# Whole first key transfer, modulation in rows, two-step picks and an early deal in a decode-attention kernel

## The chip, the cores and the metric

The kernel runs on one core of one Trainium2 chip. The time is the device time of one execution in microseconds; the median over the runs shown counts. Three runs of the kernel before gave 663.67 to 663.97, median 663.8.

## The reference

One decoding step of a transformer block with adaptive layer norm, for 4 sequences (B) and one new token each. D is 512, there are 32 heads (H) of 128 (Dh), and the caches hold 4096 keys and values for each sequence and head. All tensors are bf16.

```python
mod = (silu(c) @ w_mod).reshape(4, 6, 1, 512)          # sa, ca, ga, sb, cb, gb
h = layernorm(x) * (1 + ca) + sa
q = (h @ wq).reshape(B, 1, H, Dh).transpose(0, 2, 1, 3)
p = softmax(einsum('bhqd,bhkd->bhqk', q, k_cache) * Dh ** -0.5)
o = einsum('bhqk,bhkd->bhqd', p, v_cache)
x = x + ga * (o.reshape(B, 1, H * Dh) @ wo)
h = layernorm(x) * (1 + cb) + sb
z = gelu(h @ w_in);  z1, z2 = z[..., :896], layernorm(z[..., 896:])
x = x + gb * ((z1 * (w_sp * z2 + b_sp)) @ w_out)       # w_sp and b_sp are one number each
```

Keys and values are 134 MB each; with the weights the core reads 282.73 MB.

## The kernel before

**Stages.** The prologue loads wq and five of the six sections of w_mod, works out the modulation, the first layer norm and all queries, and spreads these so that each partition holds the query of its own head. The loop then runs over 32 sets, i = 0 to 31 (NT; L is the last, N0 = 30). Sets 0 to 29 are pairs: two sets share 8 heads of one sequence ; K and V of such a pair are 8.39 MB each, an even set and the odd one after it being the two halves of the keys. The last two sets hold four heads each of the last sequence. An epilogue projects with wo, does the second norm and the gated MLP, and writes 4 KB.

**A set.** A set has 128 keys per partition. `mult(i, 0)` and `mult(i, 1)` multiply a half of the key tile by the query in place on VectorE (L387). `reduce_d` sums over Dh with 16 matmuls against an identity on TensorE (L395), or with 4 for a part of the second half, and `sum8` finishes the sum on VectorE (L418); `sum_rest` does the remaining 48 keys on VectorE alone (L407). `scores` finds the maximum and calls `exps`, eight exponentials on ScalarE (L461) that write the weights `pbd`. `pv` multiplies them with V (64 matmuls, L516) into PSUM tile `ops`, where each partition holds results for G = 4 key groups side by side, of which a mask `sel` picks the right one: `o_pick` does this with one multiply and three multiply-adds (L525, L529). `o_cols` turns the result, `o_scale` divides by the sum of the weights and writes `oTp`.

**Buffers and the queue.** K tiles alternate between SBUF buffers A and B, V always goes into C. At the start C holds wq, w_mod and the small tiles of the prologue; so the first V load waits until the prologue has read all of them, the last being the two scalars `sp_t` (w_sp and b_sp, loaded by ScalarE's queue at L338 and L339 behind the last query copy, and read by the matmul at L362 in `late_mod_b`). SP issues all other loads, in the order of the code: wq, w_mod, K0 (two halves), K2, then V1, K4, V3, K6 and so on; a transfer named K4 holds sets 4 and 5, and V3 goes with sets 2 and 3. A V load waits for the `pv` before it, a K load for the last `sum_rest` in its buffer. At the end come wo, V30, the last V in four pieces (TAIL = 64, 32, 16, 16 keys), the last section of wo (`wol`, two halves), w_in, w_out and the last section of w_mod (`KG`, three pieces). Loads share eight semaphores, so a load also waits for the one eight places before it.

**Order.** The order of instructions on each engine is that of the code (a manual schedule). `late_mod_b` stands after the first `reduce_d` and before `mult(0, 1)`:

```python
        reduce_d(i, 0)
        ...
        if i == 0:
            late_mod_b()
        ...
        mult(i, 1)
```

`mod_cols` makes the modulation of the first two sections in columns: for each of 8 blocks, four matmuls with a strided block of w_mod as the weights. `late_mod_a` makes three more in rows (cT as the weights, 512 columns, one section on each group of 32 rows), copied to `mrows`; `late_mod_b` turns them.

**The end.** `deal(k)` spreads the `oTp` of a group of 8 heads over the partitions with eight matmuls, `dealt(k)` masks and sums on VectorE; `project` multiplies the first three groups by wo, `turn` turns the result, and `project_last` does the last group once set L is done. `o_last` runs the last V piece by piece: part 0 through `ops`, the others straight into the columns that `o_first` adds the picked part to. The epilogue's last step multiplies the MLP result `tt` by gb, whose matmuls (L872) need the last piece of w_mod.

Of the kernel before, what the change touches and what calls it, by code (L numbers as in the profile page):

```python
# [8 lines left out]
BF16 = mybir.dt.bfloat16  # L9
F32 = mybir.dt.float32  # L10
AF = mybir.ActivationFunctionType
ALU = mybir.AluOpType
AX = mybir.AxisListType
# [3 lines left out]
HP = 8  # L17
KC = 64
RD = 8
TAIL = (64, 32, 16, 16)  # L20
KIN = (slice(0, 2), slice(2, 4))
KG = (slice(0, 2), slice(2, 3), slice(3, 4))
JW = (slice(0, 4), slice(4, 7))
RW = (slice(0, 4), slice(4, 8))

# [26 lines left out]
def kernel(  # L52
# [16 lines left out]
    nc = tc.nc  # L69
    P = 128  # L70
    B, _, D = A_x.shape
# [3 lines left out]
    DJ = D // P  # L75
# [33 lines left out]
    def ps_sm(shape, dtype=F32):  # L109
        return psum.tile(shape, dtype, name="sm", bufs=3)  # L110

    def ps_q():
        return psum.tile([P, 512], F32, name="qps", bufs=1)
# [13 lines left out]
    def kv_view(cache, i):  # L127
        if i < N0:
            g, b = divmod(i // 2, B)
            v = cache[b, g * HP:(g + 1) * HP]  # L130
        else:
            h0 = GP * HP + (i - N0) * HQ
            v = cache[BL, h0:h0 + HQ]
        v = v.rearrange("h s d -> (h s) d")
        return v.rearrange("(p n) d -> p n d", p=P)
# [4 lines left out]
    def load(dst, src, cuts):  # L140
        n0 = 0
        for n in cuts:
            nc.sync.dma_start(out=dst[:, n0:n0 + n, :], in_=src[:, n0:n0 + n, :])
            n0 += n

    def load_k(i):
        if i < N0:
            load(bufs[i // 2 % 2], kv_view(A_k_cache, i), (NJ, NJ) if i == 0 else (NP,))
        else:
            load(kts[i], kv_view(A_k_cache, i), (KC, NJ - KC) if i == L else (NJ,))  # L150

    def load_v(i):
        if i < N0:
# [55 lines left out]
    def bc(ap, n):  # L209
        return ap[:, None, :].to_broadcast([P, n, ap.shape[-1]])  # L210
# [52 lines left out]
    nc.vector.reciprocal(out=sg, in_=sg)  # L263
    nc.vector.tensor_tensor(out=cT, in0=cx, in1=sg, op=ALU.mult)

    def mod_cols(s0, n, dst):

        for m in range(n):
            s, j = divmod(m, DJ)
            c0 = (s0 + s) * D + j  # L270
            for k in range(DJ):
                nc.tensor.matmul(  # L272
                    dst[:, m, :], lhsT=wm_sb[:, k, c0:c0 + (P - 1) * DJ + 1:DJ], rhs=cT[:, k, :],
                    start=(k == 0), stop=(k == DJ - 1),
                )

    xps = rows_to_cols(x_sb)
    xT = consts.tile([P, DJ, B], F32, name="xT")
# [1 line left out]
    xc1, rs1 = normed(pre, xT, "ln1")  # L280
    xn = pre.tile([P, DJ, B], F32, name="xn")
    nc.vector.tensor_tensor(out=xn, in0=xc1, in1=bc(rs1, DJ), op=ALU.mult)
    modA = ps_sm([P, 2 * DJ, B])
    mod_cols(0, 2 * DJ, modA)
    hs = pre.tile([P, DJ, B], F32, name="hs")
    nc.vector.scalar_tensor_tensor(  # L286
        out=hs, in0=modA[:, DJ:2 * DJ, :], scalar=1.0, in1=xn, op0=ALU.add, op1=ALU.mult
    )
    hT = pre.tile([P, DJ, R], BF16, name="hT")
    nc.gpsimd.memset(hT, 0.0)  # L290
    nc.vector.tensor_tensor(out=hT[:, :, 0:B], in0=hs, in1=modA[:, 0:DJ, :], op=ALU.add)

    GQ = 4
    ib = ident_bf.rearrange("p (q r) -> p r q", r=R)[:, 0:B, :, None]
# [42 lines left out]
    sp_t = pre.tile([1, 2], BF16, name="sp_t")  # L337
    nc.scalar.dma_start(out=sp_t[:, 0:1], in_=B_w_sp[0:1, 0:1])  # L338
    nc.scalar.dma_start(out=sp_t[:, 1:2], in_=B_b_sp.rearrange("(a b) -> a b", b=1))  # L339
    mrows = pre.tile([P, D], F32, name="mrows")  # L340
    nc.gpsimd.memset(mrows, 0.0)
    modT = consts.tile([P, 3 * DJ, B], F32, name="modT")
    g8 = consts.tile([P, 2, B], F32, name="g8")
    spf = consts.tile([P, 2], F32, name="spf")

    def late_mod_a():
        mp = ps_sm([P, D])
        for k in range(DJ):
            for s in range(3):
                nc.tensor.matmul(  # L350
                    mp[R * s:R * s + B], lhsT=cT[:, k, :], rhs=wm_sb[:, k, (2 + s) * D:(3 + s) * D],
                    start=(k == 0), stop=(k == DJ - 1), tile_position=(0, R * s),
                )
        for s in range(3):
            nc.scalar.copy(out=mrows[R * s:R * s + B], in_=mp[R * s:R * s + B])

    def late_mod_b():
        mps = ps_sm([P, DJ, 3 * R])
        for j in range(DJ):
            nc.tensor.transpose(mps[:, j, :], mrows[0:3 * R, j:D:DJ], ident_f[0:3 * R, 0:3 * R])  # L360
        sps = ps_sm([P, 2])
        nc.tensor.matmul(sps, lhsT=ones_b, rhs=sp_t, start=True, stop=True)  # L362
        nc.vector.tensor_copy(  # L363
            out=modT.rearrange("p (s j) b -> p s j b", s=3),
            in_=mps.rearrange("p j (s r) -> p s j r", s=3)[:, :, :, 0:B],
        )
        nc.vector.tensor_copy(out=spf, in_=sps)
        nc.gpsimd.tensor_copy(out=g8[:, 1, :], in_=spf[:, 0:1].to_broadcast([P, B]))
        cbT = modT[:, 2 * DJ:3 * DJ, :]
        nc.gpsimd.tensor_scalar_add(out=cbT, in0=cbT, scalar1=1.0)  # L370

    cbT = modT[:, 2 * DJ:3 * DJ, :]
    late_mod_a()

    st = {}
    oTp = consts.tile([P, NT // 2, HP], BF16, name="oTp")
# [120 lines left out]
    def norm_b(i):  # L497
        if (i, "z") in st:
            z = st.pop((i, "z"))
            rz = wk.tile(list(z.shape), F32, name=f"rz{z.shape[1]}", bufs=2 if pair(i) else 4)  # L500
            nc.vector.reciprocal(out=rz, in_=z)
            st[i, "rz"] = rz
# [8 lines left out]
    def pv_some(i, m0, m1, end):  # L511
        pb, vt, rows = (pbd8, bufC, G * HP) if pair(i) else (pbds[:, i % 4], vts[i], G * HQ)
        for m in range(m0, m1):
            n = slice(m * G, (m + 1) * G)
            g = R * (m % 4)
            nc.tensor.matmul(  # L516
                ops_of(i)[g:g + rows], lhsT=pb[:, n, :], rhs=vt[:, n, :],
                start=(m < 4), stop=(m >= end - 4), tile_position=(0, g),
            )

    def o_pick(i):
        ops = ops_of(i)
        sel = sels[HP if pair(i) else HQ]
        osb = wk.tile([P, DH], F32, name="osb", bufs=2)
        nc.vector.tensor_scalar(  # L525
            out=osb, in0=ops[:, 0, :], scalar1=sel[:, 0:1], scalar2=None, op0=ALU.mult
        )
        for g in range(1, G):
            nc.vector.scalar_tensor_tensor(  # L529
                out=osb, in0=ops[:, g, :], scalar=sel[:, g:g + 1], in1=osb,  # L530
                op0=ALU.mult, op1=ALU.add,
            )
        st[i, "osb"] = osb

    def o_cols(i):
# [7 lines left out]

    def o_last(i, part):
        n0, n1 = sum(TAIL[:part]), sum(TAIL[:part + 1])
        if part == 0:
            pv_some(i, 0, n1 // G, n1 // G)
            return
        if part == 1:
            st[i, "op"] = psum.tile([P, HQ], F32, name="qps", bufs=1)  # L550
        for k in range(n0, n1):
            nc.tensor.matmul(
                st[i, "op"], lhsT=vts[i][:, k, :], rhs=pbds[:, i % 4, k, :],
                start=(part == 1 and k == n0), stop=(k == NJ - 1),
            )

    def o_first(i):
# [30 lines left out]
    NL = GP * HP * DH  # L588

    def load_wo():  # L590
        nc.sync.dma_start(
            out=wo_sb.rearrange("p (k r) n -> p k r n", r=HP),
            in_=A_wo[0:NL].rearrange("(k p r) n -> p k r n", k=GP, p=P),
        )

    def load_end():
        wol = A_wo[NL:H * DH].rearrange("(p r) n -> p r n", p=P)
# [22 lines left out]
            in_=ident_bf.rearrange("p (u r) -> p r u", r=HP)[:, :, None, :].to_broadcast([P, HP, HP, P // HP]),  # L620
        )

    def deal(k):
        pp = ps_sm([P, HP, B, HP])
        for r in range(HP):
            nc.tensor.matmul(
                pp[:, r], lhsT=spot[:, r, :], rhs=oTp[:, k * B:(k + 1) * B, :], start=True, stop=True,
            )
        st["pp", k] = pp

    own = late.tile([P, HP * B, HP], F32, name="own")

    def dealt(k):
        pp = st.pop(("pp", k))
        nc.vector.tensor_tensor(
            out=own, in0=pp.rearrange("p r b h -> p (r b) h"), in1=bc(mask8, HP * B), op=ALU.mult,
        )
        od = late.tile([P, HP, B], BF16, name=f"od{k}")
        with nc.allow_low_precision("all but one term of each sum are zero"):
            nc.vector.tensor_reduce(  # L640
                out=od.rearrange("p r b -> p (r b)"), in_=own, axis=AX.X, op=ALU.add
            )
        st["od", k] = od

    accR = qbp[0:B].rearrange("b g n d -> b (g n d)")[:, 0:2 * D].bitcast(F32)

# [14 lines left out]
    def turn():  # L661
        wp = ps_sm([P, DJ, B])
        for j in range(DJ):
            nc.tensor.matmul(
                wp[:, j, :], lhsT=accR[:, j:D:DJ], rhs=ident_f[0:B, 0:B], start=True, stop=True,
            )
        return wp
# [95 lines left out]
    )  # L763
    for i in (N0, L):
        norm_b(i)
    wp = turn()
    nc.vector.tensor_tensor(out=acc, in0=wp, in1=gaT, op=ALU.mult)
    x1 = x1w[:, :, 0:B]
# [1 line left out]
    nv = NJ // G  # L770
    pv_some(N0, 0, nv // 4, nv)
    xc = centred(tl, x1, "ln2", lambda: pv_some(N0, nv // 4, nv, nv))
    o_last(L, 0)
    o_pick(N0)
    o_cols(N0)
# [4 lines left out]
    o_first(L)  # L780
    o_last(L, 3)
    o_scale(L)
    deal(GP)
    dealt(GP)
    wp = project_last()
    last = tl.tile([P, DJ, B], F32, name="last")
    nc.vector.tensor_tensor(out=last, in0=wp, in1=gaT, op=ALU.mult)
# [82 lines left out]
    for k in range(DJ):  # L870
# [23 lines left out]
    )  # L894
    tt = tl.tile([P, B, DJ], F32, name="tt")
    nc.vector.tensor_tensor(out=tt, in0=t3[:, 0], in1=t3[:, 1], op=ALU.add)
    nc.vector.tensor_scalar(
        out=t3[:, 2], in0=yb[:, 0], scalar1=spf[:, 1:2], scalar2=None, op0=ALU.mult
    )
    nc.vector.tensor_tensor(  # L900
        out=tt, in0=tt, in1=rs3[:, :, None].to_broadcast([P, B, DJ]), op=ALU.mult
    )
# [37 lines left out]
```

## Time and profile before

| | |
|---|---|
| runs, median | 663.67 to 663.97, 663.8 us |
| profiled execution | 663.61 us, span 661.8 us |
| granted TensorE clock, mean | 0.745 |
| VectorE busy | 570.6 us, 86% |
| TensorE matmul busy | 313.0 us, 47% |
| ScalarE busy | 170.9 us, 26% |
| DMA | 283.07 MB in 8188 packets, mean 428 GB/s |
| chain that ended last | DMA 62%, VectorE 21%, TensorE 11%, ScalarE 4% |
| VectorE waiting for K at L387 | 25.0 us (buffer A) and 13.6 us (buffer B) |

The span is the time from the first to the last instruction of the profiled execution; the time of the run is 1.8 us more. The chain is followed back from the last instruction to what released each step, so its shares tell where waiting was, not where an engine was busy. A row of the timeline gives start, duration, engine, line, operation, tiles and shapes, the number of instructions, and in brackets the idle time before and what ended it. A load's wait counts from its issue to its landing, so it has the time in line behind other loads in it.

### The profile page before, as it was taken

How to read it: one execution, taken by the hardware profiler on the slowest of the kernel's cores; microseconds unless marked ns; L12 is line 12 of the kernel's file. 1: busy time of each engine (PE TensorE's matmuls, PEld its weight loads, DVE VectorE, ACT ScalarE, POOL GpSimd, SP SyncE). 2: the span in 40 equal slices, each digit the busy share in tenths (PEclk: the TensorE clock that was granted, in tenths of full speed). 3: DMA queues.
4: the chain of work that ended last, by engine and by line, in shares of the span. 5: the costliest groups of instructions: out<-in, count | busy, mean ns of one | idle time of the engine just before them, and what ended most of it. 6: DMA issues, size and time to landing. Idle time of an engine off the chain costs nothing.

```text
span 661.8 us, 5160 instructions
## 1 busy us (share of the span) xinstructions
PE 313.0 (47%) x2100; PEld 134.7 (20%) x2100; DVE 570.6 (86%) x400; ACT 170.9 (26%) x282; POOL 23.9 (4%) x56
## 2 busy tenths in 40 slices
PE   1554454536153453625346361543635154363896
PEld 0221121212021121202112120111212021121345
DVE  3249999999898998989899897989989898999934
ACT  1210605032060603206060320605023060503222
POOL 3020000000000000000000000000000000030100
PEclk9988786866678786667877666787757678776876
DMA  8999999999999999999999999999999999999996
GB/s 364 449 425 444 440 441 440 441 401 440 445 428 440 437 436 416 445 436 428 437 440 433 428 440 429 424 444 440 429 432 437 424 440 445 416 415 454 412 421 280
DMA packets 8188, 283.07 MB, mean 428 GB/s; under 512 B 860, under 2 KB 1380, under 8 KB 2916
## 3 DMA queue, kind: packets, MB, share of 16 engines
q1 hardware_dynamic: 8144, 282.73, 99.0%
q8 instruction: 16, 0.26, 0.1%
q14 instruction: 8, 0.07, 0.0%
q10 hardware_dynamic: 20, 0.01, 0.0%
HBM read 282.73 MB, written 0.00 MB: 427 GB/s over the span
## 4 chain that ended last, share of the span: by engine, by line
DMA 62%; DVE 21%; PE 11%; ACT 4%; issue 1%; POOL 0%; SPq 0%; ACTq 0%; DVEq 0%
DMA bC<-in_A_v_cache_dram 34%; DMA bA<-in_A_k_cache_dram 19%; DVE bA L387 9%; DVE S L407 7%; PE ops L516 7%; DMA bC<-in_w_mod_dram 4%; DMA bC<-in_A_wo_dram 4%; ACT pbd L461 3%; PE red L395 2%; DVE S L418 2%; DMA bC<-in_B_b_sp_dram 1%; DVE bB L387 1%; PE qps L322 1%; PE sm L314 1%; DVE osb L529 0%
## 5 line engine op out<-in xcount | busy, mean ns | idle before, releaser
L461 ACT ACTIVATE pbd<-S,nb 32x256 bf16<-32x256 f32 x120 | 154.3, 1520 | 425.5 <-DVE nb L448 424.3
L387 DVE TENSOR_TENSOR bA<-bA,qbp 128x8192 bf16<-128x8192 bf16 x32 | 142.7, 4459 | 25.0 <-DMA bA<-in_A_k_cache_dram 25.0
L395 PE MATMUL red<-bB,ident_bf 128*128 128x512 bf16 x344 | 95.3, 435 | 117.5 <-DVE bB L387 117.5
L395 PE MATMUL red<-bA,ident_bf 128*128 128x512 bf16 x332 | 93.9, 442 | 116.8 <-DVE bA L387 116.8
L395 PEld LDWEIGHTS <-ident_bf 128*128 128x128 bf16 x676 | 72.5, 109 | 347.5 <-issue 183.4
L387 DVE TENSOR_TENSOR bB<-bB,qbp 128x8192 bf16<-128x8192 bf16 x28 | 123.7, 4417 | 13.6 <-DMA bB<-in_A_k_cache_dram 13.6
L516 PE MATMUL ops<-bC,pbd 128*32 128x512 bf16 x960 | 82.5, 519 | 68.8 <-DMA bC<-in_A_v_cache_dram 63.7
L407 DVE TENSOR_REDUCE S<-bA 128x48 f32<-128x6144 bf16 x15 | 98.1, 6542 | 0.0
L407 DVE TENSOR_REDUCE S<-bB 128x48 f32<-128x6144 bf16 x14 | 91.6, 6541 | 0.0
L516 PEld LDWEIGHTS <-pbd 128*32 128x32 bf16 (+1 forms) x1008 | 36.9, 125 | 116.5 <-issue 60.6
L461 ACT ACTIVATION_READ_ACCUMULATOR pbd<-S,nb 32x1 f32 x120 | 58.7, 489 | 0.0
L418 DVE TENSOR_REDUCE S<-red 128x64 f32<-128x512 f32 x64 | 43.7, 683 | 4.0 <-PE red L395 3.8
L475 POOL TENSOR_TENSOR rsb<-maskd,rs 128x8 f32<-128x8 f32 x15 | 3.9, 260 | 557.6 <-ACT pbd L461 557.6
L387 DVE TENSOR_TENSOR bB<-bB,qbo 128x8192 bf16<-128x8192 bf16 x4 | 17.6, 4410 | 0.0
L529 DVE SCALAR_TENSOR_TENSOR osb<-ops,m,osb 128x128 f32<-128x128 f32 x45 | 15.8, 351 | 1.6
L494 PE MATMUL sm<-rsb,inv_d 128*128 128x32 f32 (+2 forms) x12 | 3.1, 358 | 14.4 <-POOL rsb L475 14.4
L461 ACT ACTIVATE pbd<-S,nM 32x128 bf16<-32x128 f32 x8 | 4.6, 577 | 13.7 <-POOL pbd L707 12.5
L286 DVE SCALAR_TENSOR_TENSOR bC<-sm,bC 128x16 f32<-128x16 f32 x1 | 0.2, 175 | 8.6 <-PE sm L272 8.6
L431 DVE TENSOR_REDUCE mrow<-S 128x1 f32<-128x256 f32 (+1 forms) x17 | 6.9, 404 | 0.6
L363 DVE COPY modT<-sm 128x48 f32<-128x48 f32 x1 | 0.2, 207 | 7.3 <-PE sm L360 7.3
L322 PE MATMUL qps<-bC 128*128 128x256 bf16 (+1 forms) x16 | 4.5, 383 | 4.1 <-ACT qbp L332 2.8
L618 POOL COPY bA<-ident_bf 128x1024 bf16<-128x1024 bf16 x1 | 6.2, 6211 | 0.0
(160 smaller groups left out, 140.0 us busy)
## 6 DMA issues: line engine op xcount, KB each, us to landing
bA<-in_A_k_cache_dram SPq DMA_DIRECT2D x2, 4096.0 KB, 32.0
bC<-in_A_wq_dram SPq DMA_DIRECT2D x1, 4096.0 KB, 12.2
bB<-in_A_k_cache_dram SPq DMA_DIRECT2D x1, 4096.0 KB, 43.0
bB<-in_A_k_cache_dram SPq DMA_DIRECT2D x2, 2048.0 KB, 41.3
bA<-in_A_v_cache_dram SPq DMA_DIRECT2D x1, 4096.0 KB, 37.7
bA<-in_A_wo_dram SPq DMA_DIRECT2D x1, 3072.0 KB
bC<-in_w_mod_dram SPq DMA_DIRECT2D x1, 2560.0 KB, 17.9
bB<-in_A_v_cache_dram SPq DMA_DIRECT2D x1, 2048.0 KB
```

Source lines behind the costliest of these rows:

```text
L314: nc.tensor.matmul(qr[R * q:R * (q + 1)], lhsT=hT[:, k, :], rhs=wq_v[:, k, gs, q, :], start=(k == 0), stop=(k == DJ - 1), tile_position=(0 ...
L322: nc.tensor.matmul(qp[:, 0:npair], lhsT=eb2[k][:, b].rearrange("p k q r -> p (k q r)"), rhs=qrow[:, h, k:2 * npair:2], start=(k == 0), sto ...
L387: nc.vector.tensor_tensor(out=kt, in0=kt, in1=bc(q, KC), op=ALU.mult)
L395: nc.tensor.matmul(red, lhsT=ident_bf, rhs=kt[:, :, m * rd:(m + 1) * rd], start=(m == 0), stop=(m == DH // rd - 1),)
L407: nc.vector.tensor_reduce(out=st[i, "S"][:, n0:NJ], in_=kts[i][:, n0:NJ, :], axis=AX.X, op=ALU.add)
L418: nc.vector.tensor_reduce(out=st[i, "S"][:, kc * KC:kc * KC + on_pe(i, kc)], in_=st.pop((i, "red", kc)), axis=AX.X, op=ALU.add,)
L431: nc.vector.tensor_reduce(out=mrow, in_=S, axis=AX.X, op=ALU.max)
L461: nc.scalar.activation(out=pbd8[r, :, 2 * q + h] if pair(i) else pbds[r, i % 4, :, q], in_=S[r, :], func=AF.Exp, bias=nM[r, h:h + 1], scal ...
L475: nc.gpsimd.tensor_tensor(out=st["P", g, "rsb"][:, b], in0=maskd[:, :, None].to_broadcast([P, HQ, 2]), in1=rs[:, None, :].to_broadcast([P, ...
L516: nc.tensor.matmul(ops_of(i)[g:g + rows], lhsT=pb[:, n, :], rhs=vt[:, n, :], start=(m < 4), stop=(m >= end - 4), tile_position=(0, g),)
L529: nc.vector.scalar_tensor_tensor(out=osb, in0=ops[:, g, :], scalar=sel[:, g:g + 1], in1=osb, op0=ALU.mult, op1=ALU.add,)
L618: nc.gpsimd.tensor_copy(out=spot.rearrange("p r (a u) -> p r a u", a=HP), in_=ident_bf.rearrange("p (u r) -> p r u", r=HP)[:, :, None, :]. ...
```

## The change

The first K pair and the last K tile come in one transfer each instead of two. wo's first part comes in two transfers instead of one, the last w_mod section in four pieces instead of three. The first two modulation sections are made in rows, like the three later ones, and turned. `o_pick` multiplies `ops` by the mask in place and sums over the groups, two operations instead of four. The second piece of the last V (32 keys) joins the first on the way through `ops`. Three of the four sequences of the last head group are dealt before `turn`, the fourth at the end. One small multiplication of the epilogue (L897) moves from VectorE to ScalarE.

```diff
-KG = (slice(0, 2), slice(2, 3), slice(3, 4))
+KG = tuple(slice(k, k + 1) for k in range(4))
...
-            load(bufs[i // 2 % 2], kv_view(A_k_cache, i), (NJ, NJ) if i == 0 else (NP,))
+            load(bufs[i // 2 % 2], kv_view(A_k_cache, i), (NP,))
-            load(kts[i], kv_view(A_k_cache, i), (KC, NJ - KC) if i == L else (NJ,))
+            load(kts[i], kv_view(A_k_cache, i), (NJ,))
...
+    def mod_rows(s0, n):
+        mp = ps_sm([P, D])
+        for k in range(DJ):
+            for s in range(n):
                 nc.tensor.matmul(
-                    dst[:, m, :], lhsT=wm_sb[:, k, c0:c0 + (P - 1) * DJ + 1:DJ], rhs=cT[:, k, :],
+                    mp[R * s:R * s + B], lhsT=cT[:, k, :], rhs=wm_sb[:, k, (s0 + s) * D:(s0 + s + 1) * D],
...
+        for s in range(n):
+            nc.scalar.copy(out=mrows[R * s:R * s + B], in_=mp[R * s:R * s + B])
+    def mod_turn(n):
+        mps = ps_sm([P, DJ, n * R])
+        for j in range(DJ):
+            nc.tensor.transpose(mps[:, j, :], mrows[0:n * R, j:D:DJ], ident_f[0:n * R, 0:n * R])
+        return mps.rearrange("p j (s r) -> p s j r", s=n)[:, :, :, 0:B]
...
-    mod_cols(0, 2 * DJ, modA)
+    mod_rows(0, 2)
+    modA = mod_turn(2)
...
-        nc.vector.tensor_scalar(
-            out=osb, in0=ops[:, 0, :], scalar1=sel[:, 0:1], scalar2=None, op0=ALU.mult
+        nc.vector.tensor_tensor(
+            out=ops, in0=ops, in1=sel[:, :, None].to_broadcast([P, G, DH]), op=ALU.mult
         )
-        for g in range(1, G):
-            nc.vector.scalar_tensor_tensor(
-                out=osb, in0=ops[:, g, :], scalar=sel[:, g:g + 1], in1=osb,
-                op0=ALU.mult, op1=ALU.add,
-            )
+        nc.vector.tensor_reduce(
+            out=osb, in_=ops.rearrange("p g d -> p d g"), axis=AX.X, op=ALU.add
+        )
...
-        if part == 0:
-            pv_some(i, 0, n1 // G, n1 // G)
+        if part < 2:
+            pv_some(i, n0 // G, n1 // G, sum(TAIL[:2]) // G)
...
-        nc.sync.dma_start(
-            out=wo_sb.rearrange("p (k r) n -> p k r n", r=HP),
-            in_=A_wo[0:NL].rearrange("(k p r) n -> p k r n", k=GP, p=P),
-        )
+        wo = A_wo[0:NL].rearrange("(k p r) n -> p k r n", k=GP, p=P)
+        for ks in (slice(0, 2), slice(2, GP)):
+            nc.sync.dma_start(out=wo_sb.rearrange("p (k r) n -> p k r n", r=HP)[:, ks], in_=wo[:, ks])
...
-    def deal(k):
+    def deal(k, b0=0, b1=B):
-    def dealt(k):
+    def dealt(k, b0=0, b1=B):
...
+    deal(GP, 0, BL)
     wp = turn()
...
     xc = centred(tl, x1, "ln2", lambda: pv_some(N0, nv // 4, nv, nv))
+    dealt(GP, 0, BL)
...
-    deal(GP)
-    dealt(GP)
+    deal(GP, BL)
+    dealt(GP, BL)
...
-    nc.vector.tensor_scalar(
-        out=t3[:, 2], in0=yb[:, 0], scalar1=spf[:, 1:2], scalar2=None, op0=ALU.mult
-    )
+    nc.scalar.activation(out=t3[:, 2], in_=yb[:, 0], func=AF.Copy, scale=spf[:, 1:2])
```

More of the change, by code (lines that the diff above doesn't have):

```diff
@@ L264 @@
     nc.vector.tensor_tensor(out=cT, in0=cx, in1=sg, op=ALU.mult)
[L266 to L271, printed above, removed]
+    mrows = pre.tile([P, D], F32, name="mrows")
+    nc.gpsimd.memset(mrows, 0.0)
+    def mod_rows(s0, n):
+        mp = ps_sm([P, D])
+        for k in range(DJ):
+            for s in range(n):
                 nc.tensor.matmul(
-                    dst[:, m, :], lhsT=wm_sb[:, k, c0:c0 + (P - 1) * DJ + 1:DJ], rhs=cT[:, k, :],
-                    start=(k == 0), stop=(k == DJ - 1),
-                )
+                    mp[R * s:R * s + B], lhsT=cT[:, k, :], rhs=wm_sb[:, k, (s0 + s) * D:(s0 + s + 1) * D],
+                    start=(k == 0), stop=(k == DJ - 1), tile_position=(0, R * s),
+                )
+        for s in range(n):
[5 more added lines that the diff above has]
+        return mps.rearrange("p j (s r) -> p s j r", s=n)[:, :, :, 0:B]
     xps = rows_to_cols(x_sb)
@@ L282 @@
     nc.vector.tensor_tensor(out=xn, in0=xc1, in1=bc(rs1, DJ), op=ALU.mult)
-    modA = ps_sm([P, 2 * DJ, B])
-    mod_cols(0, 2 * DJ, modA)
+    mod_rows(0, 2)
+    modA = mod_turn(2)
     hs = pre.tile([P, DJ, B], F32, name="hs")
     nc.vector.scalar_tensor_tensor(
-        out=hs, in0=modA[:, DJ:2 * DJ, :], scalar=1.0, in1=xn, op0=ALU.add, op1=ALU.mult
+        out=hs, in0=modA[:, 1], scalar=1.0, in1=xn, op0=ALU.add, op1=ALU.mult
     )
@@ L290 @@
     nc.gpsimd.memset(hT, 0.0)
-    nc.vector.tensor_tensor(out=hT[:, :, 0:B], in0=hs, in1=modA[:, 0:DJ, :], op=ALU.add)
+    nc.vector.tensor_tensor(out=hT[:, :, 0:B], in0=hs, in1=modA[:, 0], op=ALU.add)
     GQ = 4
@@ L339 @@
     nc.scalar.dma_start(out=sp_t[:, 1:2], in_=B_b_sp.rearrange("(a b) -> a b", b=1))
-    mrows = pre.tile([P, D], F32, name="mrows")
-    nc.gpsimd.memset(mrows, 0.0)
     modT = consts.tile([P, 3 * DJ, B], F32, name="modT")
@@ L344 @@
     spf = consts.tile([P, 2], F32, name="spf")
[L346 to L352, printed above, removed]
-                )
-        for s in range(3):
-            nc.scalar.copy(out=mrows[R * s:R * s + B], in_=mp[R * s:R * s + B])
     def late_mod_b():
-        mps = ps_sm([P, DJ, 3 * R])
-        for j in range(DJ):
-            nc.tensor.transpose(mps[:, j, :], mrows[0:3 * R, j:D:DJ], ident_f[0:3 * R, 0:3 * R])
+        mps = mod_turn(3)
         sps = ps_sm([P, 2])
@@ L364, in late_mod_b @@
             out=modT.rearrange("p (s j) b -> p s j b", s=3),
-            in_=mps.rearrange("p j (s r) -> p s j r", s=3)[:, :, :, 0:B],
+            in_=mps,
         )
@@ L372 @@
     cbT = modT[:, 2 * DJ:3 * DJ, :]
-    late_mod_a()
+    mod_rows(2, 3)
     st = {}
@@ L545, in o_last @@
         n0, n1 = sum(TAIL[:part]), sum(TAIL[:part + 1])
-        if part == 0:
-            pv_some(i, 0, n1 // G, n1 // G)
+        if part < 2:
+            pv_some(i, n0 // G, n1 // G, sum(TAIL[:2]) // G)
             return
-        if part == 1:
+        if part == 2:
             st[i, "op"] = psum.tile([P, HQ], F32, name="qps", bufs=1)
@@ L553, in o_last @@
                 st[i, "op"], lhsT=vts[i][:, k, :], rhs=pbds[:, i % 4, k, :],
-                start=(part == 1 and k == n0), stop=(k == NJ - 1),
+                start=(part == 2 and k == n0), stop=(k == NJ - 1),
             )
@@ L621, in late_consts @@
         )
-    def deal(k):
-        pp = ps_sm([P, HP, B, HP])
+    def deal(k, b0=0, b1=B):
+        n = HP * (b1 - b0) * HP
+        pp = ps_sm([P, n]) if b1 == B else ps_q()[:, 0:n]
+        pp = pp.rearrange("p (r b h) -> p r b h", r=HP, h=HP)
         for r in range(HP):
             nc.tensor.matmul(
-                pp[:, r], lhsT=spot[:, r, :], rhs=oTp[:, k * B:(k + 1) * B, :], start=True, stop=True,
+                pp[:, r], lhsT=spot[:, r, :], rhs=oTp[:, k * B + b0:k * B + b1, :], start=True, stop=True,
             )
         st["pp", k] = pp
-    own = late.tile([P, HP * B, HP], F32, name="own")
-    def dealt(k):
+    mine = late.tile([P, HP * B, HP], F32, name="mine")
+    def dealt(k, b0=0, b1=B):
         pp = st.pop(("pp", k))
+        n = HP * (b1 - b0)
         nc.vector.tensor_tensor(
-            out=own, in0=pp.rearrange("p r b h -> p (r b) h"), in1=bc(mask8, HP * B), op=ALU.mult,
+            out=mine[:, 0:n], in0=pp.rearrange("p r b h -> p (r b) h"), in1=bc(mask8, n), op=ALU.mult,
         )
-        od = late.tile([P, HP, B], BF16, name=f"od{k}")
+        if b0 == 0:
+            st["od", k] = late.tile([P, HP, B], BF16, name=f"od{k}")
         with nc.allow_low_precision("all but one term of each sum are zero"):
             nc.vector.tensor_reduce(
-                out=od.rearrange("p r b -> p (r b)"), in_=own, axis=AX.X, op=ALU.add
+                out=st["od", k][:, :, b0:b1],
+                in_=mine[:, 0:n].rearrange("p (r b) h -> p r b h", r=HP), axis=AX.X, op=ALU.add
             )
-        st["od", k] = od
     accR = qbp[0:B].rearrange("b g n d -> b (g n d)")[:, 0:2 * D].bitcast(F32)
@@ L896 @@
     nc.vector.tensor_tensor(out=tt, in0=t3[:, 0], in1=t3[:, 1], op=ALU.add)
-    nc.vector.tensor_scalar(
-        out=t3[:, 2], in0=yb[:, 0], scalar1=spf[:, 1:2], scalar2=None, op0=ALU.mult
-    )
+    nc.scalar.activation(out=t3[:, 2], in_=yb[:, 0], func=AF.Copy, scale=spf[:, 1:2])
     nc.vector.tensor_tensor(
```

## Prediction, made blind

> **What bounds the kernel now.** I read the page first: the tenths of the DMA engines, the queues, then the chain of work that ended last.
>
> ```profile
> DMA  8999999999999999999999999999999999999996
> GB/s 364 449 425 444 440 441 440 441 401 440 445 428 440 437 436 416 445 436 428 437 440 433 428 440 429 424 444 440 429 432 437 424 440 445 416 415 454 412 421 280
> q1 hardware_dynamic: 8144, 282.73, 99.0%
> ```
>
> One queue, SP's, keeps the 16 DMA engines busy from 2 us to the end. 282.73 MB at this rate fill the span, so a change pays only if the stream begins earlier, moves fewer bytes or ends closer to the last instruction, and costs only if the stream runs dry or the work after it grows. The chain by time shows both ends:
>
> ```profile
> 33.76 9.16 DMA bC<-in_B_b_sp_dram
> ...
> 43.06 0.17 PE sm L362
> 43.25 0.16 DVE spf L367
> 43.41 4.34 DVE bA L387
> ...
> 82.15 5.35 PE ops L516 x64
> 87.52 29.61 DMA bC<-in_A_v_cache_dram
> 117.14 0.04 issue
> ...
> 649.09 9.21 DMA bC<-in_w_mod_dram
> 658.30 0.05 issue
> 658.35 0.28 PE sm L872 x4
> 658.65 0.18 DVE bC L904
> ```
>
> V loads land at 117.14 and 155.72 (the chain, two rows on), so 38.58 us for one V and one K of 8.39 MB: 435 GB/s, 19.3 us each. The first load, wq (4.19 MB, 12.2 us to landing on the page), met an empty queue: 4.19 MB take 9.64 us, so 2.56 us are start and landing. A V load that meets an empty queue would need 19.3 + 2.56 = 21.9 us. V3, the load issued at 87.52, took 29.61: it stood in line for **7.8 us**, and can be issued that much later for nothing. K4 (issued at 65.42, landed at 97.8) has 32.4 - 21.9 = 10.5 us, V5 33.60 - 21.9 = 11.7, V1 (issued at 43.35, landing 19.3 us after K2, which PE saw at 59.26) 13.3. V3 is the tightest place of the stream.
>
> The timeline gives the start on VectorE and the tail:
>
> ```profile
> 28.85 4.42 DVE L387 TENSOR_TENSOR bA<-bA,qbp 128x8192 bf16<-128x8192 bf16 x1 [8.01 <-DMA bA<-in_A_k_cache_dram]
> 40.58 0.21 DVE L363 COPY modT<-sm 128x48 f32<-128x48 f32 x1 [7.31 <-PE sm L360]
> ...
> 658.26 0.17 DVE L903 TENSOR_TENSOR bC<-bC 128x16 f32<-128x16 f32 x1
> 658.35 0.27 PE L872 MATMUL sm<-cT,bC 128*128 128x4 bf16 x4 [0.27 <-DMA bC<-in_w_mod_dram]
> ```
>
> At the end two things meet at L904: the sum ready at 658.43, and the last four matmuls on the last landed w_mod piece, done at 658.62. The compute chain has **0.19 us** to spare.
>
> **K0 in one transfer.** mult(0,0) started at 28.85 on the first half; it will start when all of K0 is in. mult(0,1) needed the second half, which landed at 39.87 (issue 2.7, 37.2 us to landing). So mult(0,0) runs 39.87 to 44.3. The first reduction on PE follows 4.47 us after the multiply begins (43.33 to 47.80): 44.35. Sixteen matmuls of it took 5.44 us after an idle PE (47.80 to 53.24); the gap here is 8 us, so I take that: 49.8. The four transposes of late_mod_b add 0.45 (40.10 to 40.55), the L362 matmul and the two copies 0.3: mult(0,1) at about 50.5, against 43.33. Behind the waiting copies stand all VectorE work and, through PE, the issue of V1.
>
> There is a second wait for the same place. L362 needs the two scalars sp_t, which ACT asks for after the queries, and whose pieces take turns with the big stream. x, asked for at 1.31, landed at 7.93 among 32 KB pieces (1.21 us each at 435 GB/s over 16 engines); b_sp took 9.16 us among 32 and then 64 KB pieces. In the trace's packets both waited for the piece in progress and two more, and after that one piece passed between each of their own. With K0 whole, all of these are 64 KB, 2.42 us each. Boundaries fall at 38.13 and every 2.42 after: first scalar at 42.97, and three more turns to the second's semaphore: 50.22. In the old run mult(0,1) began 0.36 after that semaphore: 50.6. So both ways give **50.6, 7.25 us later** than 43.33.
>
> From there to V3 VectorE hardly rests (33.68 busy of the 34 us from 66 to 100), and the exps and the PV follow it, so V3 is asked for at 87.52 + 7.25 = 94.8, inside its 7.8. K4 at 72.7, inside 10.5; V1 inside 13.3. VectorE works 34.3 us on a pair (65.26 to 99.56) against 38.6 of stream, so it makes up 4.3 us a pair and waits for K again by the third. Cost 0, by 0.55 us. Bounds: the reduction took 4.93 (35.17) to 5.62 us, so -0.5 to +0.2; a scalar one turn later, +2.42.
>
> The Trainium skill, Perfetto Trace Analysis, DMA Optimizations, speaks against this part: splitting a load lets work start sooner, and more so where the engines are idle. Here they are not, by the first fence; if it ruled, the 7.25 would be the price (the last rival).
>
> **Modulation in rows.** 32 matmuls (1.24 us, L272) go. In come 8 matmuls of 512 columns; the nearest row, L350, ran 12 in 1.87 us, four groups side by side, and four groups remain: 1.87. Two row copies on ACT (three took 1.75 at L355): 1.17. Four transposes (L360): 0.61. hT is 2.4 us later, and the last query copy and the scalars' issue go from 33.5 to 35.9, which the packet count above has in it. mult(0,0) waits for K0 until 39.87 anyway: 0. Without that cover it would cost 2.4.
>
> **K31 in one, wo in two, w_mod in four.** mult(31,0) starts at 613.74; the halves were issued by 560.6 and took 41.3 us, so they lay there 12 us: 0. Bytes and piece sizes of wo and w_mod stay; two issues more and two fewer, each 0.33 us on SP ahead of a backlog of 9 us. The queue waits for the transfer eight back; the last piece now waits for the second wol half instead of the first, some 1.3 us later, still 7 us before its turn: 0.
>
> **Picks.** One was 0.345 + 3 x 0.351 plus gaps, 1.51 us (643.53 to 645.04). Now a 512-element multiply and a 512-to-128 sum in PSUM; the rows show a 512-element sum at 0.683 (L418) and 256-element multiplies at 0.42. I take 0.69 + 0.04 + 0.68 = 1.41. The strided read of four terms each is not in the trace; L761, 128 elements to 32 sums, took 0.346 against 0.283 for 128 to 8 (L572): scaled by four, +0.25; the floor is the L418 row. Fifteen picks lie in the loop under waits for K of 2.6 us: 0. Two are in the tail.
>
> **Tail.** Dealing three rows early adds eight short matmuls before turn() (0.35, of which 0.23 fill PE's wait from 637.06 to 637.29): +0.15 on PE, and 0.7 of VectorE in its idle time from 641.2 to 643.5. The 32-key piece now passes through the picked path: o_pick(L) waits for eight more 512-column matmuls (16 took 1.92, so 0.96) instead of running beside them: PE ends them at 646.6, the pick at 648.05, o_first at 648.5, the last 16 keys at 648.95, against 648.35: +0.6. The last deal then has 64 elements instead of 256 in two steps of about 0.21 instead of 0.42: -0.4. L897 leaves VectorE: -0.07. Sum +0.1, inside the 0.19. Gain here can't show, since w_mod lands at 658.30. Bounds: -0.3 and +0.4 before cover, so 0 to +0.2 at the end.
>
> **Sum.** 0.0 on the profiled execution (663.61, span 661.8), which lies 0.2 under the median of 663.8. Forecast 663.8.
>
> **Rivals.** *The scalars come a turn late* (slower): mult(0,1) at 53.0, V3 9.7 us late, 1.85 past its cover, and the stream is dry that long: 665.7. It decides from 0.55 us on beyond 7.25. For it: three pieces must pass in exact turns. Against: both old scalar loads followed the count. 0.14.
>
> *PE stays slow*: after idle, nine matmuls of 47.80 came 0.43 us apart, then 0.21. If all sixteen ran at 0.43 the reduction takes 6.8, V3 is 8.6 late, 0.8 past: 664.6. Against: no row has it. 0.10. The Trainium skill, TensorE: Matmul & The Clock Gate, Part 1, has the clock halved after some 3.4 us of idleness and calls the number of slow matmuls variable from run to run.
>
> *The strided sum is slow*: at twice 0.68 the two tail picks add some 1.0 us to the +0.1, less 0.19: 664.7. No row shows it. 0.08.
>
> *Larger transfers run faster*: K0's halves took 19.36 against 19.32 for a whole K: 0.1 us over both K, 663.7; for more nothing speaks. 0.04 for a gain over 0.2%.
>
> *Compute, not the stream, sets the end*, and the late start is kept: 671.1. Against: VectorE waits 38.6 us for K (25.0 and 13.6 in the groups of L387). 0.02.
>
> **Numbers.** Forecast 0.62. The bound of 0.2% (1.3 us) is about what a measurement of this kernel can tell from no change; forecast, slow PE and slow sum lie within it: 0.80. Slower 0.16, faster 0.04. The forecast's own range is 663.4 to 664.2; with the slow cases up to the late scalars 663.3 to 665.7.
>
> **What would show it.** Right: mult(0,0) at 39.9, mult(0,1) near 50.6, V3 issued near 94.8 and landed within 0.3 us of 117.1, w_mod landed at 658.3, picks of 1.4 us. Wrong: a gap in the DMA tenths near 96 us, V3 landing late and everything after by as much; or L904 waiting for L903's chain instead of L872.

## The result and the profile after

| | median | range, runs |
|---|---|---|
| before | 663.73 us | 663.58 to 664.12, 13 |
| after | 665.18 us | 664.04 to 666.34, 13 |

The ratio is 1.0022 with a 95% interval of 1.0014 to 1.0031: slower by 1.45 us, just beyond the 1.3 us of the bound. The profiled execution of the changed kernel took 665.90 us with a span of 664.1, so it lies 0.7 us above its own median; steps read from it are a little larger than the median has them.

The page's DMA rows answer to the first fence of the prediction (40 slices of 16.6 us; DMA in tenths, then GB/s; then SP's queue).

```profile
DMA  8999999999999999999999999999999999999996
GB/s 363 478 399 435 438 431 435 434 427 415 442 439 438 434 435 438 427 422 438 439 427 435 438 442 430 424 438 438 419 442 435 442 426 427 430 430 439 418 416 241
q1 hardware_dynamic: 7888, 282.73, 98.7%
```

The same bytes, and a queue that is busy for 98.7% instead of 99.0%. No tenth drops: a gap of one or two microseconds is a tenth of a slice or less, spread over a 9. The tenths can't show what the prediction hoped to see there. It takes a window of a few microseconds, set where the trouble is expected. But first the start, on VectorE (timeline of after):

```profile
38.62 4.42 DVE L381 TENSOR_TENSOR bA<-bA,qbp 128x8192 bf16<-128x8192 bf16 x1 [14.89 <-DMA bA<-in_A_k_cache_dram]
49.70 0.21 DVE L357 COPY modT<-sm 128x48 f32<-128x48 f32 x1 [6.65 <-PE sm L283]
49.82 0.15 DVE L361 COPY spf<-sm 128x2 f32<-128x2 f32 x1
49.89 4.41 DVE L381 TENSOR_TENSOR bA<-bA,qbp 128x8192 bf16<-128x8192 bf16 x1
```

mult(0, 0) waits 14.89 us for K0 and starts at 38.62; VectorE then stands 6.65 us for the transposes of the modulation, which stand behind the first reduction on TensorE. mult(0, 1) starts at 49.89, 6.56 us later than before. This is the forecast's step with its size (50.6). The V loads follow on SP's queue (timeline of after; issue, duration of the issue):

```profile
49.90 0.33 SPq L143 DMA_DIRECT2D bC<-in_A_v_cache_dram  x1
72.16 0.33 SPq L143 DMA_DIRECT2D bA<-in_A_k_cache_dram  x1
94.28 0.33 SPq L143 DMA_DIRECT2D bC<-in_A_v_cache_dram  x1
```

They are V1, K4 and V3. V3 is issued at 94.28, 6.76 us after its 87.52 of before and even half a microsecond earlier than forecast. By the forecast's cover of 7.8 us this is free. The windows say it is not. Each row is the stretch, its length, busy us (and instructions) of PE, PEld, DVE, ACT and POOL, the granted clock, the DMA engines' share and GB/s; before first, then after.

```profile
96.00:98.50 2.50, 0.00 (x0) 0.10 (x1) 2.50 (x1) 0.00 (x0) 0.00 (x0) 0.50 1.03 446
```
```profile
96.00:98.50 2.50, 2.15 (x10) 0.88 (x9) 2.50 (x1) 0.00 (x0) 0.00 (x0) 1.00 0.67 262
```

A window counts each 64 KB piece where it starts: around the place where K4 ends and V3 begins, 10 pieces start (262 GB/s) instead of 17 (446 GB/s). That is a sign and no measure; e2 below loses more and shows 419 GB/s in the same window. The packets of the trace measure it. In before, all 16 engines always have a piece in work. In after, 13 to 15 of them do from 96.0 until 98.05, and V3's first pieces take up to 3.30 us instead of 2.42. Idle time and longer pieces together come to 0.69 us for each of the 16 engines. V3 landed at 118.02 instead of 117.14, 0.88 us late. The chain of waits shows the lateness staying (start, duration, what; after):

```profile
165.40 30.24 DMA bC<-in_A_v_cache_dram
195.64 0.04 issue
200.67 33.56 DMA bC<-in_A_v_cache_dram
234.24 0.04 issue
```

V7 and V9 land at 195.64 and 234.23; before it was 194.37 and 233.07 (161.87 + 32.50 and 199.98 + 33.09 in its chain). So they are 1.27 and 1.16 us late: what the stream loses at V3 it doesn't get back. At the end both the last V and the last w_mod piece are late (timeline of after):

```profile
650.36 0.59 PE L544 MATMUL qps<-pbd,bB 128*128 128x4 bf16 x16 [1.42 <-DMA bB<-in_A_v_cache_dram]
...
660.25 0.49 PEld L869 LDWEIGHTS <-bC 128*128 128x128 bf16 x8 [0.16 <-DMA bC<-in_w_mod_dram]
660.68 0.17 DVE L898 TENSOR_TENSOR bC<-bC 128x16 f32<-128x16 f32 x1
660.96 0.17 DVE L899 TENSOR_TENSOR bC<-bC,sm 128x16 f32<-128x16 f32 x1
```

The last piece of V lets TensorE start at 650.36 (647.79 before). From there to the end of the sum that L899 (L904 before) needs, it is 660.68 + 0.17 - 650.36 = 10.49 us, against 658.43 - 647.79 = 10.64 before. So the tail's own work did not grow. The chain of after does end in the sum (L898, done at 660.85) rather than in the last matmuls on w_mod (L869, done at 660.83), which the prediction had named as a sign of being wrong; but both are late with the loads in front of them.

The picks are rows of their own now (groups of the page: busy, mean ns of one, idle before):

```profile
L522 DVE TENSOR_REDUCE osb<-ops 128x128 f32<-128x512 f32 x17 | 11.8, 692 | 0.6
L519 DVE TENSOR_TENSOR ops<-ops,m 128x512 f32<-128x512 f32 x15 | 10.4, 693 | 0.0
```

A pick takes 0.693 + 0.692 = 1.39 us; the strided sum costs no more than the contiguous one of L418 did (0.683).

### The profile page after: what moved, and what is told of

It reads as the page before. It is cut to its first block, busy times and chain, and to the rows that moved or that the text cites. A ratio compares the mean times of both kernels' runs of the same rounds, so it can differ in the third digit from the quotient of the medians.

```text
span 664.1 us, 5061 instructions
## 1 busy us (share of the span) xinstructions
PE 316.2 (48%) x2064; PEld 133.5 (20%) x2064; DVE 570.6 (86%) x367; ACT 172.2 (26%) x285; POOL 23.8 (4%) x56
## 3 DMA queue, kind: packets, MB, share of 16 engines
q1 hardware_dynamic: 7888, 282.73, 98.7%
## 4 chain that ended last, share of the span: by engine, by line
DMA 57%; DVE 28%; PE 11%; ACT 2%; issue 1%; SPq 0%; ACTq 0%; DVEq 0%
DMA bC<-in_A_v_cache_dram 35%; DMA bA<-in_A_k_cache_dram 18%; DVE bA L381 10%; DVE S L401 10%; PE ops L510 7%; DMA bB<-in_A_v_cache_dram 5%; DVE bB L381 4%; PE red L389 4%; DVE S L412 2%; ACT pbd L455 2%; DVE osb L522 0%; DVE ops L519 0%; DVE mrow L425 0%; PE red L835 0%; PE sm L670 0%
## 5 line engine op out<-in xcount | busy, mean ns | idle before, releaser
L389 PE MATMUL red<-bA,ident_bf 128*128 128x512 bf16 x332 | 96.2, 450 | 120.5 <-DVE bA L381 120.5
L522 DVE TENSOR_REDUCE osb<-ops 128x128 f32<-128x512 f32 x17 | 11.8, 692 | 0.6
L519 DVE TENSOR_TENSOR ops<-ops,m 128x512 f32<-128x512 f32 x15 | 10.4, 693 | 0.0
L273 PE MATMUL sm<-bC,cT 128*4 128x512 bf16 x20 | 3.7, 621 | 8.3 <-DMA bC<-in_w_mod_dram 8.3
```

Source lines behind the costliest of these rows:

```text
L273: nc.tensor.matmul(mp[R * s:R * s + B], lhsT=cT[:, k, :], rhs=wm_sb[:, k, (s0 + s) * D:(s0 + s + 1) * D], start=(k == 0), stop=(k == DJ - ...
L389: nc.tensor.matmul(red, lhsT=ident_bf, rhs=kt[:, :, m * rd:(m + 1) * rd], start=(m == 0), stop=(m == DH // rd - 1),)
L519: nc.vector.tensor_tensor(out=ops, in0=ops, in1=sel[:, :, None].to_broadcast([P, G, DH]), op=ALU.mult)
L522: nc.vector.tensor_reduce(out=osb, in_=ops.rearrange("p g d -> p d g"), axis=AX.X, op=ALU.add)
```

## The experiments

The theory (A in the expectations): VectorE's late start makes V3 late on the queue, and the queue runs partly dry although V3 is issued before K4 is done. Its rivals: the end of the kernel lost the time (B), picks and rows in the loop did (C), or the whole transfer's 64 KB pieces did by themselves (D). Each kernel was measured beside the kernel before, which gave 663.73 us (27 runs) beside the first four and 663.82 (33 runs) beside the other four; ratios are to these. Each experiment has 11 runs, e4 has 5.

**e1: the whole change, but K0 in halves.**

```diff
-            load(bufs[i // 2 % 2], kv_view(A_k_cache, i), (NP,))
+            load(bufs[i // 2 % 2], kv_view(A_k_cache, i), (NJ, NJ) if i == 0 else (NP,))
```

> The changed kernel with one part undone: the first K pair comes in two halves again. Theory A (the late start on VectorE makes V3 reach the queue too late, and the stream loses time there): 663.7, V3 issued within 1 us of 87.5 and landed within 0.3 of 117.1. Theory B (the new tail, where the 32-key piece goes through the picked path, ends later than the last load): still 665.0 to 665.4. Theory C (the picks or the rows of modulation cost along the loop): 665.0 or more.

Measured: 663.90 us, ratio 1.0002 (0.9993 to 1.0010). The loss is gone, and with it B and C: rows, picks, the other transfers, the early deal and L894 on ScalarE cost nothing that can be measured. A detail of the expectation missed: V3 was issued at 91.72 instead of within 1 us of 87.5. The timeline of e1 on VectorE shows why:

```profile
42.30 0.21 DVE L357 COPY modT<-sm 128x48 f32<-128x48 f32 x1 [8.86 <-PE sm L283]
48.16 0.16 DVE L361 COPY spf<-sm 128x2 f32<-128x2 f32 x1 [5.65 <-PE sm L356]
48.23 4.42 DVE L381 TENSOR_TENSOR bA<-bA,qbp 128x8192 bf16<-128x8192 bf16 x1
```

The transposes were done by 42.30, but mult(0, 1) stood 5.65 us more for the two scalars, which ScalarE asks for behind the queries, 2.9 us later than before (the first at 36.36 instead of 33.48). So with K0 in halves the modulation in rows already starts mult(0, 1) 4.9 us and V3 4.2 us later than before. That was still free.

**e2: the kernel before, with K0 whole and nothing else.** The edit is the reverse of e1's, on the old kernel.

> The kernel before with one part of the change alone: the first K pair in one transfer. Theory A: mult(0,1) starts at about 49.9, V3 is issued at 94.2, the stream behind it is late by 0.5 to 1.3 us, 665.0 to 665.4 with a spread of 2 us. Theories B and C: 663.7.

Measured: 665.80 us, ratio 1.0028 (1.0019 to 1.0037): slower by 2.07. One line of the change is enough. Here K0 landed 1.1 us later than in the changed kernel (mult(0, 0) at 39.70), V3 was issued at 95.21, and V9 landed at 235.47, 2.40 us late. About half of that comes from V3: V5 is 1.27 us late, K8, the load behind it, 2.51.

**e3: the whole change with K0 whole, and the copies of the modulation moved behind mult(0, 1).**

```diff
         reduce_d(i, 0)
         ...
-        if i == 0:
-            late_mod_b()
         ...
         mult(i, 1)
+        if i == 0:
+            late_mod_b()
```

> The changed kernel, first K pair whole, but late_mod_b stands behind mult(0,1), so that the multiplication does not wait for the first reduction and the transposes. Theory A: mult(0,1) starts at about 43.1, V3 is issued near 89.5, 663.7. Theory D (not the delay, but the transfer itself is to blame, by its 64 KB pieces at the start of the stream): 665.2 as with the change. Theory B: 665.2.

Measured: 663.57 us, ratio 0.9997 (0.9989 to 1.0006). VectorE runs the two multiplications of K0 back to back as soon as K0 is in (timeline of e3, two instructions in one row):

```profile
38.50 8.76 DVE L381 TENSOR_TENSOR bA<-bA,qbp 128x8192 bf16<-128x8192 bf16 x2 [14.88 <-DMA bA<-in_A_k_cache_dram]
```

V3 goes out at 90.48, and the window in which the changed kernel starved is full again (window of e3):

```profile
96.00:98.50 2.50, 0.00 (x0) 0.10 (x1) 2.50 (x1) 0.00 (x0) 0.00 (x0) 1.00 1.03 446
```

K0 is whole here with all its 64 KB pieces, so D falls. What cost the time is the order in which VectorE's wait for the transposes stands ahead of mult(0, 1).

**e4: only the delay.** The kernel before, with nothing changed but 14 idle fills of a spare tile on VectorE ahead of mult(0, 1).

```diff
+    pause = ps_q()
...
         if i == 0:
             late_mod_b()
+            for _ in range(14):
+                nc.vector.memset(pause, 0.0)
```

> The kernel before, all of it, with 14 idle fills of an unused PSUM tile (0.49 us each by L708) on VectorE ahead of mult(0,1): the delay of 6.8 us without any part of the change. Theory A: V3 issued near 94.2, 665.0 to 665.4 and a wide spread. Theories B, C and D: 663.7, since the prediction's cover of 7.8 us would hold.

Measured: 667.07 us, ratio 1.0048 (1.0034 to 1.0061). The fills came 0.67 us apart, not 0.48, so V3 was delayed by 9.8 us instead of 6.8, to 97.31. That is past the forecast's cover of 7.8 too, so this run doesn't decide between it and a smaller one. But with K0 in halves, old picks and the old tail, delay alone costs 3.34 us (665.38 to 668.38). In this window hardly a piece starts (window of e4), and from 97.5 to 98.0 two of the 16 engines have one in work:

```profile
95.00:98.00 3.00, 2.61 (x38) 1.13 (x31) 3.00 (x2) 0.00 (x0) 0.00 (x0) 0.88 0.13 49
```

**e5, e6, e7: the same with 6, 8 and 10 fills**, to find where it begins to cost.

> The kernel before with 6 fills ahead of mult(0,1), each taking 0.67 us from start to start as in the run with 14: 4.1 us of delay, V3 issued at about 91.6. If a load must be issued some 4.5 us before the queue runs out (theory A with the lead that the first runs show: no stretched pieces at a lead of 4.6 us, nearly all at 1.8): at the edge, 663.7 to 663.9. If the prediction's cover of 7.8 us held: 663.7.

> As above with 8 fills, 5.4 us, V3 issued at about 92.9, lead 3.2 us. Theory A with the longer lead: 664.1 to 664.8. With a cover of 7.8 us: 663.7.

> As above with 10 fills, 6.8 us, V3 issued at about 94.3, as in the changed kernel, with none of the change in it. Theory A: 665.0 to 665.6. With a cover of 7.8 us: 663.7. If something of the change adds to the loss: below the changed kernel's 665.2.

Measured: 663.77 (ratio 1.0001, 0.9993 to 1.0010), 664.28 (1.0010, 1.0001 to 1.0018) and 664.95 (1.0016, 1.0007 to 1.0025). Ten fills are 10 x 0.67 = 6.7 us, inside the cover of 7.8, and the median loses 1.13 us. Single runs differ widely: 663.65 to 666.30 with 8 fills, 663.67 to 665.60 with 10. In the profiled execution of e7 the scalars came early (V1 was issued at 41.27, against 43.35 before), and V3 went out at 91.31 in spite of ten fills; that execution took 663.72. Its trace belongs to the free cases; the median is probably of other, later starts, which no trace shows.

**e8: the whole change with V3 in halves**, so that its first half may go out once half of the PV before it is done.

```diff
-            load(bufC, kv_view(A_v_cache, i), (NP,))
+            load(bufC, kv_view(A_v_cache, i), (NJ, NJ) if i == 3 else (NP,))
```

> The changed kernel with V3 alone in two transfers, so that its first half is issued when half of the pv before it is done, at about 91.7 instead of 94.3; VectorE is as late as with the change. Theory A, and V3 the only place where the stream loses: 663.6 to 663.9. If the late VectorE also costs elsewhere (K4, V5, or the end): 664.2 or more.

Measured: 663.86 us, ratio 1.0003 (0.9995 to 1.0012). The first half was issued at 91.30, the second at 93.0. VectorE starts about as late as in the changed kernel (V1 goes out at 49.10 and 49.90), and in the median the loss is gone, though two of the 11 runs took 665.10 and 665.26. So the late issue of V3 is what costs the time.

**Side by side.** From each profiled execution: when V3 was issued (SP's rows); the engine time lost around V3, which is, from the packets between 94 and 100.5 us, the time without a piece and the time of pieces beyond their usual 2.42 us (1.21 for 32 KB), for each of the 16 engines; when TensorE first used K6, the load behind V3; when V9 landed (chain); and that execution's time.

| kernel | V3 issued | lost around V3 | K6 in use | V9 landed | profiled time |
|---|---|---|---|---|---|
| before | 87.52 | 0.00 | 136.47 | 233.07 | 663.61 |
| e3 | 90.48 | 0.00 | 136.51 | 232.97 | 663.44 |
| e5 | 91.03 | 0.00 | 136.75 | 233.30 | 663.99 |
| e8 (first half) | 91.30 | 0.03 | 136.65 | 232.97 | 663.79 |
| e7 | 91.31 | 0.04 | 136.75 | 233.19 | 663.72 |
| e1 | 91.72 | 0.03 | 136.54 | 232.99 | 663.53 |
| e6 | 93.58 | 0.19 | 136.50 | 233.81 | 664.28 |
| after | 94.28 | 0.69 | 137.93 | 234.23 | 665.90 |
| e2 | 95.21 | 1.10 | 137.73 | 235.47 | 665.96 |
| e4 | 97.31 | 2.39 | 140.66 | 237.14 | 667.61 |

The rows of K6 in before, e6 and after (timelines; PEld is TensorE's weight load):

```profile
136.47 0.10 PEld L395 LDWEIGHTS <-ident_bf 128*128 128x128 bf16 x1 [7.64 <-DMA bB<-in_A_k_cache_dram]
136.50 0.10 PEld L395 LDWEIGHTS <-ident_bf 128*128 128x128 bf16 x1 [2.07 <-DMA bB<-in_A_k_cache_dram]
137.93 0.10 PEld L389 LDWEIGHTS <-ident_bf 128*128 128x128 bf16 x1 [2.35 <-DMA bB<-in_A_k_cache_dram]
```

Up to 93.58 little is lost and K6 is on time; at 94.28 each engine loses 0.69 us and K6 is 1.46 us late. The true cover of V3 therefore lies, in these executions, between 93.58 - 87.52 = 6.06 and 94.28 - 87.52 = 6.76 us. In before, thirteen of V3's 16 first pieces start between 95.71 and 96.09, so a load issued 2.1 us ahead of that was free, and one 1.4 us ahead was not.

V9 and the time hold more than V3's part. A load has landed when the last of its 16 engines is done, so one engine that falls behind makes it late. In e6 this happens well after V3: V5 lands at 155.76 (155.72 before) and K8 at 175.91 (175.07 before), with the second last engine at 175.06. What held that one engine was not tested.

## Why the prediction was wrong

**What bounds the kernel: right.** One stream, V3 as its tightest place, and every microsecond lost there kept to the end.

**mult(0, 1) at 50.6, V3 near 94.8: right**, at 49.89 and 94.28, partly by luck in the terms. K0 landed at 38.52 instead of 39.87, and the reduction took longer than the 5.44 taken for it (PE's groups in the timeline of after, start, duration, what, idle before):

```profile
43.10 6.12 PE L389 MATMUL red<-bA,ident_bf 128*128 128x512 bf16 x16 [4.97 <-DVE bA L381]
49.05 0.61 PE L283 MATMUL sm<-ident_f,bC 96*128 96x96 f32 x4
49.59 0.17 PE L356 MATMUL sm<-bC 1*128 1x2 bf16 x1
```

6.12 us lies between the 5.44 of the forecast and the 6.8 of the rival "PE stays slow"; the transposes took 0.54 to the L356 matmul. The second way to 50.6, by the scalars, did not come out by its count: their second semaphore came at 48.01, about one turn of a 64 KB piece ahead of the counted 50.22. So the wait was TensorE's alone, and the rival "the scalars come a turn late" did not happen.

**The cover of 7.8 us: the step that failed.** It was worked out as 29.61 - 21.9 from V3's landing, with 2.56 us for a load's start and landing, from wq on an empty queue. The table puts it between 6.06 and 6.76: the term was 1.0 to 1.7 us too large, and the 6.76 us of delay, inside the forecast's cover by 1.0, lay at or past the end of the true one. The 21.9 itself was not far off: V3 of e4, which met nearly idle engines, took 119.77 - 97.31 = 22.46. What the term left out is most likely that a landing tells of the last engine. In before, fourteen of the 16 engines have done their share of K4 1.4 to 1.8 us ahead of its landing at 97.82, and from then on they need V3. 7.8 less that is 6.0 to 6.4, an estimate that fits the table. K4 in e4 says the same: it was issued 75.21 - 65.42 = 9.8 us late, inside its forecast cover of 10.5, and still each engine lost 0.7 us at its place (packets from 75 to 80 us). No run tests this reading by itself.

The size of the loss is less well known than its place. The changed kernel lost 0.69 us for each engine around V3, with K6 1.46 late and V9 1.16; the profiled time is 2.29 up and the median 1.45. The prediction did name the mechanism in its rival with the late scalars, V3 past its cover and the stream dry for as long, but it gave that rival a delay that did not occur, and never put a bound on the cover itself. A range for 7.8 from a single row met in another situation would have moved much of the 0.80 for "no change" to "slower".

**The rule that spoke against the change.** The Trainium skill, Perfetto Trace Analysis, DMA Optimizations, says that splitting a load may let part of it start sooner, and may end the whole task sooner if the engines are generally idle. The prediction set it aside because they are busy. The trace agrees with that rule in direction: K0 in halves instead of whole is worth 665.18 - 663.90 = 1.28 us between after and e1. It does not come as the 7.25 us of a late start that the last rival priced, but through the lead of a later load.

**Modulation in rows at 0: right in the time, too confident.** The queries end 2.9 us later, not 2.4 (36.36 and 33.48, above), and in e1 V3 is issued 4.2 us later. Some 2 us of its cover were left behind that. The two delays do not add: K0 whole alone (e2) takes 7.7 us of the cover, with the rows (after) 6.8. The copies ahead of mult(0, 1) wait for whichever is last, the scalars or the transposes, and in both kernels it was the transposes; K0 landed 1.1 us later in e2.

**Picks, K31, wo, w_mod, the early deal: right.** Picks 1.39 us for a forecast of 1.41, and no penalty for the stride, so "the strided sum is slow" falls. The last deal took 0.22 + 0.22 for a forecast of two steps of 0.21. The tail was put at +0.1 and was 10.49 - 10.64 = -0.15; the +0.6 of the 32-key piece did not come, since in e1, where the loads are on time, the last `oTp` is written at 648.35 against 648.38 before. e1 and e3, which have all of these parts, are within 0.1% of before.

**What stays open.** V9 is 1.16 us late in after, and the profiled execution 2.29 us slow: the K load issued at 522.63 lands 1.28 late (564.12 against 562.84 in the chains), the last V 2.5. The spread of the 16 engines grows on the way: they finish V29 within 3.9 us of each other, against 3.0 before, and of the lateness of the last V some 1.4 us is one engine's, lost between 643.9 and 654.9. Short transfers of 16 KB that fetch program code hold single engines for some 0.9 us at times that differ between runs (one starts at 648.3 in after, one at 646.4 in before) and could do this; which engine they meet is not in the trace, and no run tested it. So V3's place accounts for the loss, but not for all of its size, nor for the wider spread of the changed kernel's runs (2.3 us against 0.5).

## What to carry to other kernels

On a queue that is kept full, the slack of a load is not its time in line less a start-up taken from an empty queue; it is the lead over the moment at which the first engines need it, less what the start takes. A landing time tells only of the last engine, so the slack is best measured by delaying the load on purpose, as the idle fills did here. When a transfer is made whole for the sake of fewer pieces, look at what stands behind its first use in program order: moving two small copies behind the next multiplication (e3, 663.57 us) kept all of the change at the time of before, though its 0.16 us of gain lies within its interval.

## What the runs showed of the hardware

A load that is issued ahead of the end of the one before it can still leave the engines short. V3 at 94.28 was issued 1.4 us before its first pieces' place at 95.71, and up to three of the 16 engines stood without a piece until 98.05, while its first 64 KB pieces took up to 3.30 us instead of 2.42. At 93.58, 2.1 us ahead, five pieces were long, and at 91.72 one. In e4, where V3 met engines that had run out, its first pieces start 0.97 us after the start of its issue (97.31 to 98.28) and take 2.62 to 3.39 us. The Trainium skill, DMA: Bandwidth & Descriptors, Latency and other measured facts, gives about 0.6 us to a transfer's first byte on the hardware queues. The 0.97 us less the 0.33 us of the issue itself comes close to that, and the lead that was needed is two to three times as much.

The 16 engines pass from one load to the next at different moments: in before, fourteen finish K4 1.4 to 1.8 us ahead of the last. So a late load meets some engines idle and others still at work, and the loss around V3 grows with the delay, from 0.69 us for each engine at 94.28 to 1.10 at 95.21 and 2.39 at 97.31.
